# One load queue and a new order of steps in a linear-attention plus Mish feed-forward kernel

## The chip, the cores and the metric

The kernel runs on one core of a Trainium2 chip. The metric is the device time of one execution in microseconds, the median of the runs. A core has a matrix engine (TensorE, PE in the profile; PEld is its weight load), VectorE (DVE), ScalarE (ACT), GpSimd (POOL) and a sync engine (SP), which here only issues DMAs. ScalarE can issue DMAs too. SP and ScalarE each have a DMA queue of their own. Each engine carries out its own instructions in the order in which they were written and waits on semaphores for the others.

## The reference

```python
xn = layernorm(x)                                   # x: 2048 x 448, no gain or bias
q, k, v = split(xn @ wqkv)                          # 16 heads of 28
pq, pk = q @ w_phi, k @ w_phi                       # per head, 28 x 28
phi_q = concat(softmax(pq), softmax(-pq))           # 56 features per head
phi_k = concat(softmax(pk), softmax(-pk))
kv, z = phi_k.T @ v, sum(phi_k)                     # over all 2048 rows
o = (phi_q @ kv) / (phi_q @ z + 1e-6)
h = xn @ w1 + b1                                    # 448 -> 1792
out = x + o @ wo + mish(h) @ w2                     # mish(h) = h * tanh(softplus(h))
```

Inputs and output are bfloat16.

## The kernel before, in words

The 2048 rows are 16 tiles of 128 (t = 0 to 15), worked on in 8 pairs (u = t // 2). Everything stays in on-chip memory: x, the weights, the activations (actT) and exp(k), which lies in the half of actT that the second half of the feed-forward writes later.

The kernel is a list of steps. Each step has a short name and a function; the string ORDER names all steps in the order in which they are recorded, and a small recorder (Program) turns that list into one instruction list per engine, with a semaphore wait wherever a step reads or overwrites what another engine or a DMA produces. So ORDER alone decides the order of work on every engine and in every DMA queue. The last letter of some names says where a step runs: a for ScalarE, d for VectorE, p for POOL, m for a DMA transpose, s for SP's queue.

The steps, in the order of the data:

- Loads: lxA.Bs/a loads x tiles A to B-1; lkm and lvm the first 384 rows of the k and v columns of wqkv; lkt, in before, the last 64 rows of both, twice, to the lower and to the upper 64 partitions (Wkv[:, 3]); lqT0 to lqT3 the q columns by DMA transpose (WqT); lp w_phi (Wbd), lb b1, l1m and l1t w1, l2 w2, lo wo.
- Layer norm: stT statistics, rs (a pair) or rtT (a tile) the reciprocal deviation, xnT the normalised tile into one of four buffers xn0 to xn3, xtU the transpose of a pair into xnT. With xtUb or xtUa TensorE transposes and ScalarE and/or VectorE copy out; with xtUm a DMA does it.
- Folding w_phi into the projections: wtk0 and wtk1 turn the k weights on TensorE (L547), wmk0 and wmk1 multiply them by Wbd (L571) and copy the result to Wpk; qd copies the end of WqT once more, and wmq0, wmq1 make Wpq from it.
- Projections of a pair: kU, qU, vU. Each is 14 matmuls in three passes, A, B and H; two matmuls of 64 rows run side by side. A unit holds a pair of the eight PSUM banks until its result is copied out: exp(k) and exp(-k) by ScalarE (L609), exp(q) likewise (L682), v by ScalarE or VectorE (the copies all show as L509 or L511).
- Key normalisation: knU.S, a row sum and reciprocal on VectorE (L617, L619) and a scaling on POOL (L621) for each sign; kcU does the sum of both signs in one instruction (L627).
- kvU: 16 matmuls of a pair into kv, accumulated over all pairs; kvz masks the result and a DMA transposes it (KVZ). It needs all 16 scalings by POOL.
- eT transposes exp(q) of tile T by DMA (EqT); ndT makes numerators and denominators on TensorE, then a chain of seven VectorE instructions; otU transposes the result back.
- Feed-forward: fQ.C is half Q (tiles 0 to 7, or 8 to 15) of chunk C of w1, 14 matmuls in passes A, B and H, then Mish on ScalarE with another activation table (L703). gT is the product with w2, 14 matmuls (L828); wo the output projection (L845); a VectorE sum with x (L793) and stoU, sttT the stores.
- z12: 12 matmuls on zeros at the very start. pi, pw, pp, pv, pk: constants, masks and paddings by POOL.

Of the kernel before, what the change touches and what calls it, by code (L numbers as in the profile page):

```python
# [171 lines left out]
def _kernel(es, nc, A_x, A_wqkv, A_w_phi, A_wo, B_w1, B_b1, B_w2, out):  # L172
# [363 lines left out]
    def w_tr(h, eng):  # L536
# [7 lines left out]
        def tr(e):  # L544
            for c in range(2):
                for g in range(G):
                    ins = e.transpose(oT(c)[:, g, :], Wk[:, 2 * h + c, g * GP:(g + 1) * GP], ident[:])  # L547
# [432 lines left out]
```

## Time and profile before

| | |
|---|---|
| median of 3 runs | 153.9 us (153.81 to 154.15) |
| profiled execution | 153.96 us, of which the span of its instructions is 152.2 us |
| TensorE busy | 144.6 us (95%), 1541 matmuls |
| VectorE busy | 101.1 us (66%) |
| ScalarE busy | 75.7 us (50%) |
| POOL busy | 44.3 us (29%), all of it before 57 us |
| DMA moved | 17.22 MB, mean 113 GB/s |
| TensorE clock granted | 1.00 |

How to read it: shares are means over stages with different limits, and a busy TensorE says little where matmuls follow each other with waits that the modelled ends cover. What counts in a stage is the chain of work: which wait ended last there. Rows of the timeline merge instructions of one kind: start, time from the first start to the last end, how many; in brackets the idle time of the engine before and what ended it.

### The profile page before, as it was taken

How to read it: one execution, taken by the hardware profiler on the slowest of the kernel's cores; microseconds unless marked ns; L12 is line 12 of the kernel's file. 1: busy time of each engine (PE TensorE's matmuls, PEld its weight loads, DVE VectorE, ACT ScalarE, POOL GpSimd, SP SyncE). 2: the span in 40 equal slices, each digit the busy share in tenths (PEclk: the TensorE clock that was granted, in tenths of full speed). 3: DMA queues.
4: the chain of work that ended last, by engine and by line, in shares of the span. 5: the costliest groups of instructions: out<-in, count | busy, mean ns of one | idle time of the engine just before them, and what ended most of it. 6: DMA issues, size and time to landing. Idle time of an engine off the chain costs nothing.

```text
span 152.2 us, 3611 instructions
## 1 busy us (share of the span) xinstructions
PE 144.6 (95%) x1541; PEld 76.1 (50%) x1541; DVE 101.1 (66%) x223; ACT 75.7 (50%) x90; POOL 44.3 (29%) x65
## 2 busy tenths in 40 slices
PE   3978999989999979999999999999999999999993
PEld 1454545445444574445344455554544554559552
DVE  0699989599969903599606999535995999200721
ACT  3485999995995699778997730000500400000000
POOL 3385688969999950000000000000000000000000
PEclk9999999999999999999999999999999999999999
DMA  5995964989967243994399260500035000540204
GB/s 123 288 260 147 174 143 93 131 268 262 101 137 138 76 139 73 180 197 41 60 149 321 86 65 14 119 0 0 2 65 151 30 4 0 121 121 4 87 4 151
DMA packets 40436, 17.22 MB, mean 113 GB/s; under 512 B 34020, under 2 KB 39908, under 8 KB 40420
## 3 DMA queue, kind: packets, MB, share of 16 engines
q1 hardware_dynamic: 37548, 14.46, 46.9%
q10 hardware_dynamic: 2872, 2.53, 5.6%
q8 instruction: 12, 0.20, 0.5%
q14 instruction: 4, 0.03, 0.1%
HBM read 7.02 MB, written 1.84 MB: 58 GB/s over the span
## 4 chain that ended last, share of the span: by engine, by line
PE 78%; ACT 12%; DMA 4%; DVE 3%; issue 1%; ACTq 0%
PE PS L429 38%; PE PS L828 28%; PE PS L845 7%; DMA x_all<-in_A_x_dram 4%; ACT actT L609 3%; PE PS L723 2%; PE PS L650 2%; ACT actT L682 2%; ACT v_all L509 2%; DVE Sk L627 1%; ACT Wpq L509 1%; ACT Eq L682 1%; DVE v_all L511 1%; ACT Eq L509 1%; ACT Wpk L509 1%
## 5 line engine op out<-in xcount | busy, mean ns | idle before, releaser
L703 ACT ACTIVATE actT<-PS,b1T 128x1024 bf16<-128x1024 f32 x28 | 30.2, 1112 | 33.1 <-PE PS L429 33.0
L429 PE MATMUL PS<-xnT,W 64*128 64x512 bf16 x392 | 46.2, 376 | 0.0
L828 PE MATMUL PS<-W,actT 128*128 128x448 bf16 (+1 forms) x224 | 42.7, 351 | 0.0
L828 PEld LDWEIGHTS PS<-W,actT 128*128 128x128 bf16 x224 | 21.5, 98 | 20.3 <-issue 0.7
L429 PEld LDWEIGHTS PS<-xnT,W 64*128 64x128 bf16 x392 | 18.1, 94 | 21.0 <-ACT actT L703 0.4
L793 DVE TENSOR_TENSOR x_all<-PS,x_all 128x448 bf16<-128x448 f32 (+1 forms) x16 | 9.5, 616 | 20.3 <-PE PS L845 10.3
L621 POOL TENSOR_TENSOR actT<-actT,rSk 128x896 bf16<-128x896 bf16 x12 | 20.0, 1699 | 0.0
L609 ACT ACTIVATE actT<-PS 128x896 bf16<-128x896 f32 x16 | 13.7, 950 | 3.7 <-DVE stats L466 1.8
L429 PE MATMUL PS<-Wkv,xnT 64*128 64x448 bf16 x112 | 13.6, 349 | 0.6 <-DVE v_all L511 0.6
L429 PE MATMUL PS<-Wpk,xnT 64*128 64x448 bf16 x112 | 13.3, 349 | 0.5 <-ACT Wpk L509 0.5
L429 PE MATMUL PS<-Wpq,xnT 64*128 64x448 bf16 x112 | 12.7, 350 | 0.0
L466 DVE BATCH_NORM_STATS2 stats<-x_all 128x6 f32<-128x448 bf16 x15 | 9.2, 614 | 5.2 <-DMA x_all<-in_A_x_dram 5.2
L617 DVE TENSOR_REDUCE Sk<-actT 128x32 f32<-128x896 bf16 x12 | 12.5, 1043 | 0.0
L738 DVE COPY Sq<-PS 128x16 f32<-128x16 f32 x32 | 4.0, 167 | 12.5 <-PE PS L723 12.2
L749 DVE TENSOR_TENSOR xn<-v_all,rden 128x448 bf16<-128x448 f32 x16 | 10.0, 625 | 1.3 <-DMA Wkv<-xn 0.8
L746 DVE TENSOR_TENSOR v_all<-v_all 128x464 f32<-128x464 f32 x16 | 10.3, 642 | 0.6
L742 DVE TENSOR_TENSOR v_all<-PS,Sq 128x464 f32<-128x464 f32 x16 | 10.3, 642 | 0.5
L744 DVE TENSOR_TENSOR v_all<-PS,Sq 128x464 f32<-128x464 f32 x16 | 10.1, 630 | 0.0
L429 PEld LDWEIGHTS PS<-Wkv,xnT 64*128 64x128 bf16 x112 | 5.4, 94 | 6.0 <-DVE v_all L511 1.0
L682 ACT ACTIVATE actT<-PS 128x896 bf16<-128x896 f32 x10 | 8.4, 926 | 0.0
L429 PEld LDWEIGHTS PS<-Wpk,xnT 64*128 64x128 bf16 x112 | 5.3, 94 | 5.5 <-ACT Wpk L509 0.6
L429 PEld LDWEIGHTS PS<-Wpq,xnT 64*128 64x128 bf16 x112 | 5.1, 94 | 5.4 <-ACT actT L609 0.5
(85 smaller groups left out, 137.7 us busy)
## 6 DMA issues: line engine op xcount, KB each, us to landing
W<-in_B_w_dram SPq DMA_DIRECT2D x1, 1568.0 KB, 8.0
out_dram<-x_all SPq DMA_DIRECT2D x7, 224.0 KB, 2.2
W<-in_B_w_dram SPq DMA_DIRECT2D x1, 1344.0 KB, 7.2
x_all<-in_A_x_dram ACTq DMA_DIRECT2D x5, 224.0 KB, 4.1
Wo<-in_A_wo_dram ACTq DMA_DIRECT2D x2, 336.0 KB, 3.6
x_all<-in_A_x_dram SPq DMA_DIRECT2D x2, 224.0 KB, 4.9
W<-in_B_w_dram SPq DMA_DIRECT2D x2, 224.0 KB, 4.0
Wkv<-in_A_wqkv_dram SPq DMA_DIRECT2D x1, 336.0 KB, 4.2
```

The costliest lines, as they stand in the source:

```text
L429: ins = e.matmul(o, lhs(c, k), rhs(c, k), start=first and n == at[par][0], stop=last and n == at[par][-1])
L609: op("ACT", lambda e, s=s: e.activation(E_of(u)[:, s, :, :], two(b, D), ACT.Exp, scale=1.0 if s == 0 else -1.0), r=[pb(b), pb(b + 1)], w=[ ...
L617: op("DVE", lambda e: e.tensor_reduce(Sk[u][:, s, :], Eh(), AX.X, ALU.add), r=[("E", u, s)], w=[("Sk", u, s)], tag=f"Sk{u}.{s}")
L621: op("POOL", lambda e: e.tensor_tensor(Eh(), Eh(), ap_on(rSk[u][:, s, 0:1], [[1, 2 * H], [0, DH]]), ALU.mult), r=[("E", u, s), ("rSk", u, ...
L682: op("ACT", lambda e, s=s: e.activation(Eq_of(u)[:, :, s, :].rearrange("p i (h n) -> p i h n", n=64)[:, :, :, 0:QP], two(b, D).rearrange(" ...
L703: op("ACT", lambda e: e.activation(actT[:, q, fc, :], bank(b, 2), ACT.Mish, bias=b1T[:, fc:fc + 1]), r=[("b1T",), pb(b), pb(b + 1)], w=[(" ...
L742: op("DVE", lambda e: e.tensor_tensor(tv(t1[i]), num(0), sx(1), ALU.mult), r=[pb(b), pb(b + 1), ("Sq", i, 1)], w=[("t1", i)], tag=f"ta{t}")
L744: op("DVE", lambda e: e.tensor_tensor(tv(t2), num(1), sx(0), ALU.mult), r=[pb(b), pb(b + 1), ("Sq", i, 0)], w=[("t2",)], tag=f"tb{t}")
L746: op("DVE", lambda e: e.tensor_tensor(t1[i], t1[i], t2, ALU.add), r=[("t1", i), ("t2",)], w=[("t1", i)], tag=f"tc{t}")
L749: op("DVE", lambda e: e.tensor_tensor(o_sb[(t // 2) % 2][:, t % 2, :].rearrange("p (h d) -> p h d", d=DH), t1[i][:, :, 0:DH], ap_on(rden[i ...
L828: ins = e.matmul(bank(b)[:, 0:width(t)], act_of(fc, t), W2[:, fc, 0:width(t)], start=first and fc == 0, stop=last and fc == FC - 1)
L845: ins = e.matmul(bank(b)[:, 0:w], oT_of(u)[lo:hi, cc * P:(cc + 1) * P], Wo[lo:hi, cc, 0:w], start=first and n == at[par][0], stop=last and ...
```

## The change

Three edits, and a part that is only defined.

1. The tail of the weights. Before, the last 64 rows of the k and v columns came twice, 64 partitions of 896 columns each. Now the lower half gets k and v, the upper half v alone, and the turning of the k weights (w_tr, second half) takes the tail from the lower 64 partitions twice: eight transposes of 64 rows to 64 columns in place of four of 128 rows to 128 columns.
2. The queues. All loads of x, the k, v and q weights, w1, w2 and wo are in SP's queue; b1 and w_phi in ScalarE's.
3. ORDER is new as a whole.

New functions center, center_T, minus_rstd, v_early, k_early and q_early are defined and given step names (xc, ct, nr, v..e, v..f, k..c, q..c), of which none is in the new ORDER; tok_works, x_res, early_of serve them.

```diff
-pi lx1.2a pw table lx0.1s lx4.6a lx2.4a zero st1d lpa st5a st0d st4d st2d rs0p lvma rs2p lx6.8a xn0a xn1d lkms xn5p
-lkts xn4p lx8.10s lbs st3d z12 wtk0a rt2a wtk1d xt0b lqT3 rt3a wmk0d wmk1a pp b1 xt2b xn2d st8d lqT1 lqT2 lqT0 xn3d
...
+lx1.2s lx2.4s lx0.1s pw pi lx4.8s zero table pp z12 st1d st0d rs0p st2d lba st4d lkms xn1d rt4p lkts lpa st3a lvts
+st5a rt5a lvms xn0d xn4d b1 lx10.12s rs1p wtk0a lx12.14s xt0a lx8.10s xn5d wtk1d wmk0d xn3d lqT3 xt2b wmk1a xn2d lqT0
...
+    def load_kv_tail(i, eng):
+        lo, hi = HALF[i]
+        dst, src = (Wv, A_wqkv[384:448, 2 * D:3 * D]) if i else (Wkv, A_wqkv[384:448, D:3 * D])
+        dma(eng, lambda e: e.dma_start(dst[lo:hi, 3, :], src), w=[("Wt", i)], tag=f"ldWt{i}")
...
-        return [(name, 0), ("Wt", 0), ("Wt", 1)] if name in ("Wk", "Wv") else [(name, i) for i in range(3)]
+        return [(name, 0), ("Wt", 0)] + ([("Wt", 1)] if name == "Wv" else []) if name in ("Wk", "Wv") else \
+            [(name, i) for i in range(3)]
...
-                    ins = e.transpose(oT(c)[:, g, :], Wk[:, 2 * h + c, g * GP:(g + 1) * GP], ident[:])
+                    for lo, hi in HALF if h and c else ((0, P),):
+                        ins = e.transpose(oT(c)[:, g, lo:hi], Wk[0:hi - lo, 2 * h + c, g * GP:(g + 1) * GP],
+                                          ident[0:hi - lo, 0:hi - lo])
...
-        add(f"lkt{c}", load_tail, eng, "Wkv", Wkv, A_wqkv[:, D:3 * D])
+        for i, n in enumerate("kv"):
+            add(f"l{n}t{c}", load_kv_tail, i, eng)
```

What the new order does on the engines is shown at four places; the line numbers of the kernel after are its own. First SP's queue from its first load on, before:

```order
L273 DMA x_all<-in_A_x_dram 128x448
L276 DMA Wkv<-in_A_wqkv_dram 128x3x448
L281 DMA Wkv<-in_A_wqkv_dram 64x896 x2
L273 DMA x_all<-in_A_x_dram 128x896
L303 DMA b1_rows<-in_B_b1_dram 14x128
L285 DMA_TRANSPOSE WqT<-in_A_wqkv_dram 128x448 x4
L516 DMA_TRANSPOSE xnT<-xn1 128x7x128
```

And after:

```order
L286 DMA x_all<-in_A_x_dram 128x448
L286 DMA x_all<-in_A_x_dram 128x896
L286 DMA x_all<-in_A_x_dram 128x448
L286 DMA x_all<-in_A_x_dram 128x1792
L289 DMA Wkv<-in_A_wqkv_dram 128x3x448
L300 DMA Wkv<-in_A_wqkv_dram 64x896
L300 DMA Wkv<-in_A_wqkv_dram 64x448
L289 DMA Wkv<-in_A_wqkv_dram 128x3x448
L286 DMA x_all<-in_A_x_dram 128x896 x3
L303 DMA_TRANSPOSE WqT<-in_A_wqkv_dram 128x448 x4
L535 DMA_TRANSPOSE xnT<-xn1 128x7x128
```

The k weights move from second place to fifth, behind 896 KB of x, and the q weights' transposes stand behind eleven loads. Further on in SP's queue, behind the next three xnT transposes, the kernel before has two more of them and then the main part of w1; after, two transposes of exp(q) come first:

```order
L535 DMA_TRANSPOSE xnT<-xn0 128x7x128
L780 DMA_TRANSPOSE EqT<-actT 128x8x128 x2
L535 DMA_TRANSPOSE xnT<-xn1 128x7x128
L535 DMA_TRANSPOSE xnT<-xn3 128x7x128
L289 DMA W1<-in_B_w1_dram 128x3x1792
```

The two EqT rows are tiles 3 and 2 (pair 1); the two xnT rows behind them pairs 5 and 7.

Second, ScalarE from its first copy of turned key weights (Eq0) to the first exp(k) (L609), before, its DMA issues among them:

```order
L509 ACTIVATE Eq0<-PS 112x1024
L478 ACTIVATE lnv<-mv,eps_col 128x1
L480 ACTIVATE rstd<-lnv 128x1
L509 ACTIVATE xnT<-PS 128x384
L478 ACTIVATE lnv<-mv,eps_col 128x1
L480 ACTIVATE rstd<-lnv 128x1
L509 ACTIVATE Wpk<-PS 128x896
L509 ACTIVATE xnT<-PS 128x384
L273 DMA x_all<-in_A_x_dram 128x896 x2
L609 ACTIVATE actT<-PS 128x896 x2
```

And after (L699 is the first exp(k); L477 to L481 are the statistics of a tile, here tile 6):

```order
L528 ACTIVATE Eq0<-PS 112x1024
L528 ACTIVATE xnT<-PS 128x896
L528 ACTIVATE xnT<-PS 128x384
L528 ACTIVATE Wpk<-PS 128x896
L477 ACTIVATE junk1,mv<-x_all 128x448
L479 ACTIVATE rmean<-mv 128x1
L481 ACTIVATE junk1,mv<-x_all,rmean 128x448
L528 ACTIVATE v_all<-PS 128x32x28
L699 ACTIVATE actT<-PS 128x896 x2
```

Two pairs of logarithm and exponential for rstd left the stretch between Eq0 and Wpk; a set of statistics and the copy of v of pair 0 came in ahead of the first exp(k).

Third, TensorE from the turning of the key weights to the folding of q, before:

```order
L547 MATMUL PS<-ident,Wkv 112x128 x16
L504 MATMUL PS<-ident,xn 128x128 x7
L571 MATMUL PS<-Wbd,Eq 128x112 x16
L695 MATMUL PS<-ident,b_rows 128x14
L504 MATMUL PS<-ident,xn 128x128 x7
L429 MATMUL PS<-Wpk,xnT 128x448 x22
L429 MATMUL PS<-Wkv,xnT 128x448 x28
L571 MATMUL PS<-Wbd,WqT 128x112 x16
```

And after:

```order
L567 MATMUL PS<-ident,Wkv 112x128 x8
L523 MATMUL PS<-ident,xn 128x128 x7
L567 MATMUL PS<-ident,Wkv 112x128 x4
L567 MATMUL PS<-ident,Wkv 112x64 x8
L592 MATMUL PS<-Wbd,Eq 128x112 x8
L523 MATMUL PS<-ident,xn 128x128 x7
L592 MATMUL PS<-Wbd,Eq 128x112 x8
L448 MATMUL PS<-Wkv,xnT 128x448 x8
L448 MATMUL PS<-Wpk,xnT 128x448 x8
L448 MATMUL PS<-Wkv,xnT 128x448 x8
```

The first projection on TensorE is now v (Wkv) and not k (Wpk), and the two transposes of x stand between the halves of the key weights.

Fourth, POOL from the last of its mask steps (KVT) over its last normalised tile to its first scalings of exp(k), before:

```order
L354 MEMSET KVT 128x512
L498 TENSOR_SCALAR xn1<-x_all,rstd,shift 128x64
L498 TENSOR_SCALAR xn1<-x_all,rstd,shift 128x384
L621 TENSOR_TENSOR actT<-actT,rSk0 128x896 x2
L621 TENSOR_TENSOR actT<-actT,rSk1 128x896
L633 TENSOR_TENSOR actT<-actT,rSk3 128x896 x2
```

And after, from the last normalised tile to the first mask step (mask2):

```order
L517 TENSOR_SCALAR xn3<-x_all,rstd,shift 128x64
L517 TENSOR_SCALAR xn3<-x_all,rstd,shift 128x384
L711 TENSOR_TENSOR actT<-actT,rSk2 128x896
L711 TENSOR_TENSOR actT<-actT,rSk1 128x896
L711 TENSOR_TENSOR actT<-actT,rSk0 128x896
L711 TENSOR_TENSOR actT<-actT,rSk1 128x896
L364 MEMSET mask2 128x56
```

The mask steps moved behind the first four scalings. The order of the kv groups on TensorE is now pairs 4, 2, 0, 3, 1, 6, 7, 5 (before 2, 6, 1, 0, 5, 7, 4, 3), and ahead of them stand seven q units and a part of an extra feed-forward chunk (f0.1), where before the last q unit came after them. The copies of v of pairs 3, 4 and 5 went from VectorE to ScalarE, that of pair 7 from ScalarE to VectorE.

More of the change, by code (lines that the diff above doesn't have):

```diff
@@ new lines, in minus_rstd, with sign_rstd, v_early, then @@
+    def minus_rstd(u):
+        op("DVE", lambda e: e.tensor_scalar(nrstd[:, 2 * u:2 * u + 2], rstd[:, 2 * u:2 * u + 2], -1.0, 0.0, op0=ALU.mult, op1=ALU.add),
+           r=[("rstd", 2 * u), ("rstd", 2 * u + 1)], w=[("nr", u)], tag=f"nr{u}")
+    def sign_rstd(t, s):
+        return nrstd[:, t:t + 1] if s else rstd[:, t:t + 1]
+    def v_early(u, part, eng):
+        def then(b):
+            for i in range(2):
+                t = 2 * u + i
+                dst, src = v_all[:, u, i, :, 0:DH], bank(b + i)[:, 0:D].rearrange("p (h d) -> p h d", d=DH)
+                r, w = [pb(b + i), ("rstd", t)], [("v", u)] if i else [("vh", u)]
+                if eng == "ACT":
+                    op("ACT", lambda e, dst=dst, src=src, t=t: e.mul(dst, src, rstd[:, t:t + 1]), r=r, w=w, tag=f"vs{u}.{i}")
+                else:
+                    op("DVE", lambda e, dst=dst, src=src, t=t: e.tensor_scalar(dst, src, rstd[:, t:t + 1], 0.0, op0=ALU.mult,
+                                                                               op1=ALU.add), r=r, w=w, tag=f"vs{u}.{i}")
+        pair_part(f"v{u}", part, tok_works(u, Wv, True), x_res(u, True) + rows_of("Wv"), then)
@@ new lines, in k_early, with then @@
+    def k_early(u, part):
+        def then(b):
+            for s in range(2):
+                for i in range(2):
+                    t = 2 * u + i
+                    op("ACT", lambda e, s=s, i=i, t=t: e.activation(E_of(u)[:, s, i, :], bank(b + i)[:, 0:D], ACT.Exp,
+                                                                    scale=sign_rstd(t, s)),
+                       r=[pb(b + i), ("rstd", t), ("nr", u)], w=[("E", u, s)] if i else [("Eh", u, s)], tag=f"exkc{u}.{s}.{i}")
+        pair_part(f"k{u}", part, tok_works(u, Wp[1], True),
+                  x_res(u, True) + [("Wp", 1, h, c) for h in range(2) for c in range(2)], then)
@@ new lines, in q_early, with then @@
+    def q_early(u, part):
+        def then(b):
+            for s in range(2):
+                for i in range(2):
+                    t = 2 * u + i
+                    op("ACT", lambda e, s=s, i=i, t=t: e.activation(
+                        Eq_of(u)[:, i, s, :].rearrange("p (h n) -> p h n", n=64)[:, :, 0:QP],
+                        bank(b + i)[:, 0:D].rearrange("p (h n) -> p h n", n=QP), ACT.Exp, scale=sign_rstd(t, s)),
+                       r=[pb(b + i), ("Eqp", u % 3), ("rstd", t), ("nr", u)], w=[("Eq", u % 3, s)],
+                       tag=f"exqc{u}.{s}.{i}")
+        pair_part(f"q{u}", part, tok_works(u, Wp[0], True), x_res(u, True) + [("Wp", 0, c) for c in range(4)], then)
@@ L903, in _kernel @@
                 add(f"f{q}.{fc}{part}", ffn1, q, fc, part)
+    for u in range(4):
+        add(f"nr{u}", minus_rstd, u)
+        for eng, c in (("ACT", "a"), ("DVE", "d"), ("both", "b")):
+            add(f"ct{u}{c}", center_T, u, eng)
+        for part in "ABH":
+            add(f"v{u}{part}e", v_early, u, part, "ACT")
+            add(f"v{u}{part}f", v_early, u, part, "DVE")
+            add(f"k{u}{part}c", k_early, u, part)
+            add(f"q{u}{part}c", q_early, u, part)
+        for t in (2 * u, 2 * u + 1):
+            add(f"xc{t}d", center, t, "DVE")
+            add(f"xc{t}p", center, t, "POOL")
     add("kvz", kvz)
```

72 lines of the change are left out of this document (52 added, 20 removed).

## The prediction

> **What bounds the kernel now.** I read the page's shares first, then the chain of work that ended last, then the timeline of each engine where that chain leaves TensorE. The page and the chain, in order of time (start us, us, what):
>
> ```profile
> PE 144.6 (95%) x1541; PEld 76.1 (50%) x1541; DVE 101.1 (66%) x223; ACT 75.7 (50%) x90; POOL 44.3 (29%) x65
> PE 78%; ACT 12%; DMA 4%; DVE 3%; issue 1%; ACTq 0%
> ...
> 8.93 0.91 ACT Eq L509
> 9.84 0.19 ACT lnv L478
> ...
> 11.06 0.81 ACT Wpk L509
> ...
> 11.92 4.17 PE PS L429 x42
> ...
> 17.83 1.75 ACT Wpq L509 x4
> 19.58 3.24 ACT actT L609 x4
> ...
> 23.22 3.30 ACT actT L682 x4
> ...
> 28.14 0.81 ACT v_all L509
> ...
> 30.60 2.03 DVE Sk L627
> ...
> 33.20 0.96 DVE v_all L511
> ...
> 34.21 18.73 PE PS L429 x184
> 52.94 3.17 PE PS L650 x124
> 56.10 0.78 issue
> 56.88 0.29 PE PS L650 x4
> ...
> 149.27 0.56 DVE x_all L793
> ```
>
> Three parts. To 11.92 a serial start: x lands, is normalised, the key weights are folded (L547, L571), ScalarE moves them out (Wpk). From 11.92 to 34.2 ScalarE carries the chain, with a detour over VectorE at its end. From 34.2 TensorE runs without a break except the pause before the last kv group at 56.10. So time can come from an earlier start, from pauses before 57, and from nothing after 57 unless an edit adds a pause: TensorE's work is the same in both kernels, apart from the turned tail.
>
> Rates for what follows, from the timeline:
>
> ```profile
> 21.83 3.00 PE L429 MATMUL PS<-Wpq,xnT 64*128 64x448 bf16 x30
> 46.05 3.40 PE L429 MATMUL PS<-xnT,W 64*128 64x512 bf16 x30
> 34.21 0.74 PE L429 MATMUL PS<-Wkv,xnT 64*128 64x448 bf16 x6 [0.59 <-DVE v_all L511]
> 7.17 1.17 PE L547 MATMUL PS<-ident,Wkv 128*112 128x128 bf16 x16
> 9.90 0.96 PE L571 MATMUL PS<-Wbd,Eq 112*128 112x112 bf16 x16 [0.34 <-ACT Eq L509]
> 42.00 1.28 ACT L703 ACT_TABLE_LOAD   x1
> 45.03 9.99 POOL L621 TENSOR_TENSOR actT<-actT,rSk 128x896 bf16<-128x896 bf16 x6
> ```
>
> With a modelled end of 0.17 taken off a merged row, 30 matmuls of 448 take 2.83, so a k, q or v unit of 14 takes 1.32 (an A or B pass 0.57, H 0.19); a feed-forward unit of 14 matmuls of 512 takes 1.51. A kv group is 16/124 of 3.17 = 0.41. One POOL scaling of exp(k) is 1.67.
>
> **The change part by part.**
>
> *Dead code.* The new functions (center, v_early, k_early, q_early, minus_rstd) have no step in the order table, so no engine gets an instruction from them; early_of only names resources that nothing else writes. Cost 0.
>
> *Loads.* All loads of x and of the k and v weights now stand in SP's queue; ScalarE's keeps b1 and the four w_phi pieces. Wo's four loads move to SP too, behind the transpose of tile 6, some 30 us before the first wo: 0.
>
> ```profile
> 0.00:4.00 4.00, 1.70 (x5) 0.60 (x6) 0.37 (x1) 1.28 (x1) 1.35 (x10) 1.00 0.53 134
> 4.00:8.00 4.00, 4.00 (x22) 1.95 (x21) 2.66 (x8) 1.63 (x5) 1.68 (x4) 1.00 1.17 277
> 8.00:12.00 4.00, 2.55 (x40) 1.96 (x39) 3.90 (x14) 3.76 (x9) 2.73 (x7) 1.00 0.84 228
> x_all<-in_A_x_dram SPq DMA_DIRECT2D x1, 112.0 KB, 2.6
> Wkv<-in_A_wqkv_dram SPq DMA_DIRECT2D x1, 336.0 KB, 4.2
> 4.09 5.10 SPq L285 DMA_TRANSPOSE WqT<-in_A_wqkv_dram x4
> xnT<-xn SPq DMA_TRANSPOSE x6, 3.8
> ```
>
> The last columns of the first three rows are the clock, DMA share and GB/s. At these rates 536 KB have moved by 4.0 and 1,644 by 8.0. In the new order x tiles 0 to 7 are the first 896 KB: moved by 5.3, landed with some 0.5 of lag by 5.8. The key weights follow at 1,232 KB: 6.5, landed 7.0. That is 1.5 later than before (issued at 1.27, 4.2 to land), but TensorE could not use them earlier, since its warm-up runs to 7.17. The tail of V alone saves 56 KB, 0.2 of the queue. The bulk ends at 2,408 KB, landed near 11.9. SP's own issue is longer: eleven loads near 0.5, then four transposes of 1.27 (5.10/4) from about 6.2 to 11.3; the last would land near 14 to 15.5, and xT of pair 1, behind it, is issued when xn2 is ready at 11.7. [...] The rows leave the landing between 14 and 15.5; I take the middle, where nothing waits.
>
> *The turned tail.* Four transposes of 128 rows become eight of 64 rows. No row shows that shape; by the 16 above (0.063 from start to start) it costs between 0 and 4 x 0.063 = 0.25. I take 0.25. It lies under ScalarE's copy of the first half of the turned weights (0.91), which the next product needs anyway; uncovered it would cost 0.25.
>
> *The start, walked through.* x1 lands near 3.3, x2 and x3 by 3.8, x0 by 4.2, x4 to x7 by 5.8. ScalarE now takes the statistics of tiles 3 and 5.
>
> ```profile
> 5.42 0.58 ACT L458 ACTIVATE junk<-x_all 128x448 bf16<-128x448 bf16 x1 [2.87 <-DMA x_all<-in_A_x_dram]
> 6.92 0.19 ACT L462 ACTIVATION_READ_ACCUMULATOR junk<-x_all,rmean 128x1 f32 x1
> 24.75 1.07 DVE L617 TENSOR_REDUCE Sk<-actT 128x32 f32<-128x896 bf16 x1
> 27.11 5.01 POOL L621 TENSOR_TENSOR actT<-actT,rSk 128x896 bf16<-128x896 bf16 x3
> W<-in_B_w_dram SPq DMA_DIRECT2D x1, 1344.0 KB, 7.2
> ```
>
> One such set is 5.42 to 7.11 = 1.69: tile 3 from 3.85, tile 5 from 5.8 to 7.5, its logarithm and rstd (0.42, the two small steps of the chain) to 7.95. TensorE: warm-up to 7.17, first half of the key weights turned by 7.9, xT of pair 0 by 8.3, second half by 8.9. ScalarE: the turned half 7.95 to 8.85, xT of pair 0 to 9.75 (896 columns, taken as that same 0.9), xT of pair 2 to 10.3, Wpk 10.35 to 11.16. Between Eq and Wpk the chain of before has two pairs of ln and rstd, 0.8 in all; they are gone from this place, and that is where the start becomes earlier. TensorE: 9.75 to 10.13 the second product; then v of pair 0, which needs no folded weight, 10.13 to 10.9; then k of pair 0 at 11.2. Before, the stream began with k at 11.92 and v came after it. Start term: 1.8 earlier less the 0.35 hole = -1.45.
>
> *To the kv groups.* From k at 11.2 on TensorE has 23 units less the two v passes (29.6), six feed-forward units and the H and B passes of f0.1 (9.9) and the folding of q (16 matmuls, 0.8): 40.3, so kv could begin at 51.5. The same count for before gives 11.92 + 39.7 = 51.6, where the chain shows 52.94: 1.3 of waiting, of which the 0.59 behind the VectorE copy of v3 is the piece with a name. That copy stood behind a double reduction (2.03) which waited for exp(k3); in the new order ScalarE does v3 and no double reduction is left (two single ones take 2 x (1.07 + 0.35), less overlaps about the same as the double's 2.03 + 0.55). ScalarE allows it: exp of k0 begins 13.75, and counting 1.62 a pair (3.24/2), 0.82 a v and the two remaining Wpq copies it ends exp(k5) near 38.8 with all eight k, four q and five v, where before it came to the table load behind that work at 42.00, with one v fewer. What is late next: xT of pair 4 (issued 21.3 when POOL has done xn8, 3.8 to land: 25.1, wanted 25.1) and q4, whose bank waits for the copy of v4 (31.5, wanted 31.5).
>
> *The kv groups.* VectorE goes without a break from 9.5 (its steps to the first key sum add up to 14.2) and reaches it at 23.8 instead of 24.75; POOL begins at 25.15 instead of 27.11. It then has 16 x 1.67 and, now among them, the mask steps (2.2): 54.1. TensorE finishes the sixth group at 51.5 + 6 x 0.41 = 53.95, waits 0.15 for the seventh, ends the eighth at 54.9. Before: 57.17.
>
> *After that.* Before has 149.27 - 57.17 = 92.1 to the last sums. The new order has already done q3's A pass and 0.86 of f0.1, 1.4 more, so 90.7 are left: 54.9 + 90.7 = 145.6. I went through the waits there.
>
> ```profile
> 65.89 0.26 DVE L738 COPY Sq<-PS 128x16 f32<-128x16 f32 x2
> ...
> 66.73 0.63 DVE L744 TENSOR_TENSOR v_all<-PS,Sq 128x464 f32<-128x464 f32 x1
> ...
> 68.91 0.25 DVE L738 COPY Sq<-PS 128x16 f32<-128x16 f32 x2
> ```
>
> An nd chain takes VectorE 3.0 (65.89 to 68.91) and gives its bank back after 1.45; the tightest place is g10, which wants the bank of nd12 (0.5 spare). No new pause. The end is of the same form (g15, its sums, two stores).
>
> *Sum.* With no pause that I did not count: 145.6 against 149.27, -3.65. Before lost 1.3 + 0.95 on pauses in a stream with as many crossings between engines; five places of the walk above have less than 0.3 to spare. Between none of that and all of it (2.25) I take half: +1.1. Result -2.55 on the profiled execution (153.96, its span 152.2), which stands 0.06 above the median of 153.9: 151.4.
>
> **The rivals.**
>
> *POOL gives the lead back.* If VectorE is not ahead, POOL starts at 27.1 as before and ends its 28.9 at 56.0; kv ends 56.8, the end is 147.5: -1.8, with some 0.5 of small pauses 152.7. For it: VectorE is full from 9.5 on, any late x tile moves it. Against: even then most of the reordering stays.
>
> *The start does not move* (loads hidden anyway, ScalarE's chain as long as before): -3.65 + 1.45 + 1.1 = -1.1, 152.9. Against: the two ln/rstd pairs are out of the chain.
>
> *The clock falls back.*
>
> ```profile
> 2.31 5.03 PE L370 MATMUL PS<-zeros 128*128 128x512 bf16 x12 [2.31 <-POOL zeros L322]
> ```
>
> The warm-up's 12 matmuls take 0.42 each, twice the 0.216 that a pair of 512 columns costs later, though the clock column reads 1.00 there too. Between 7.2 and 11.2 the walk leaves TensorE pauses of some 0.7. If these let it fall back to the speed of the warm-up for about as long as that lasted (2.31 to 7.17, 4.9), half of it is lost: 2.4, so 153.8. Against: before had larger holes there, 1.45 idle between 8 and 12, and stayed fast. [...]
>
> *Slower: W1 behind the queue.* On SP, two transposes of exp(q1) now stand ahead of xT of pairs 5 and 7 and of W1's main part, and wait for exp(q1). I have that at 22.5, W1 issued at 27.6 and landed 7.2 later, 35.4 (unless it shares the queues), wanted at 36.5. All TensorE work stands behind it. If exp(q1) ends at 26.5 as before, W1 lands at 39.4, 2.9 too late: -2.55 + 2.9 is +0.35, the point from which this decides; with the two transposes landing beside it 1 more, 155. Against: exp(q1) is one place earlier in ScalarE's list.
>
> **How the numbers follow.** Forecast 0.57, POOL 0.15, start unmoved 0.11, clock 0.06, W1 0.11. What a measurement of this kernel can tell from no change is about 0.2%, 0.3 us. Faster: 0.57 + 0.15 + 0.11 = 0.83; same: the clock, 0.06; slower 0.11. The range goes from the sum with no uncounted pause (153.96 - 3.65 = 150.3) over POOL and the unmoved start to just short of the clock's case, 153.5.
>
> **What the profile after would show.** Right: key weights turned from about 7.2, first v matmul at 10.1 and first k at 11.2; POOL's first scaling near 25; kv ends near 55 to 56; no TensorE idle over 0.3 between 12 and 50; full from 57 to the last sums near 146.7. Wrong: a TensorE wait on a DMA of xnT or W1 between 20 and 37; the WqT double copy on VectorE held past 15.2 by the last WqT load; POOL starting at 27 or later; a clock below 1.00 after 7; a pause in the nd part.

## The result, and the profile after

The new kernel takes 155.94 us (median of 18 runs, 154.10 to 157.47); the kernel before, on the same chips, 153.91 us (153.45 to 154.34). The forecast was 151.4 us, so faster; it is slower, by 1.3% from median to median. The ratio 1.0053 (95% interval 1.0033 to 1.0074) leaves out, as disturbed, the nine runs whose mean granted clock was 0.978; the experiments below show that this clock is the new kernel's own doing, so the median of all runs is the figure to go by.

The 18 runs fall into three groups by their mean clock: 1.00 (four runs, mean 154.2), 0.989 (five, 155.2) and 0.978 (nine, 157.0). The profiled execution is one of the middle group: 155.42 us, span 153.5.

The shares of the chain on the page of the kernel after:

```profile
PE 84%; DMA 7%; DVE 6%; SPq 1%; issue 1%; DVEq 0%
```

The chain in order of time (start us, us, what):

```profile
2.66 6.42 DMA Wkv<-in_A_wqkv_dram
9.13 0.90 PE PS L567 x8
10.03 0.75 PE PS L523 x7
10.78 1.31 PE PS L567 x12
12.09 0.86 PE PS L592 x8
12.97 1.09 DVE Wpk L530
...
21.16 3.88 DMA xnT<-xn
25.04 0.14 issue
25.18 30.72 PE PS L448 x310
55.90 3.33 PE PS L740 x128
59.23 6.38 PE PS L448 x58
...
150.58 0.56 DVE x_all L883
```

ScalarE, which carried the chain of the kernel before from 16.11 to 30.60, is gone from it. The chain now has one long DMA near its start, the key weights, 6.42 us from issue to landing; after 12.97 it follows VectorE's list to the transpose that lands at 25.04. TensorE was held by that second part for 0.19 only, as its own rows show (in the bracket the idle time ahead of them), and by the first for 2.15:

```profile
9.13 0.90 PE L567 MATMUL PS<-ident,Wkv 128*112 128x128 bf16 x8 [2.15 <-DMA Wkv<-in_A_wqkv_dram]
...
13.66 0.93 PE L448 MATMUL PS<-Wkv,xnT 64*128 64x448 bf16 x8
14.73 0.55 PE L448 MATMUL PS<-Wpk,xnT 64*128 64x448 bf16 x4
...
25.18 0.36 PE L448 MATMUL PS<-Wpk,xnT 64*128 64x448 bf16 x2 [0.19 <-DMA xnT<-xn]
```

The first v comes at 13.66 (forecast 10.13), the first k at 14.73 (11.2; before 11.92). After that the only pause before the kv groups is 0.19. The table by stage has clock, DMA share and GB/s in its last columns:

```profile
4.00:8.00 4.00, 2.98 (x10) 1.03 (x8) 1.85 (x5) 1.98 (x6) 0.96 (x2) 1.00 0.92 249
8.00:12.00 4.00, 2.87 (x27) 2.69 (x27) 2.27 (x9) 3.62 (x9) 1.81 (x4) 0.67 1.28 283
12.00:16.00 4.00, 3.85 (x46) 2.55 (x47) 3.68 (x9) 2.57 (x6) 0.00 (x0) 0.90 0.44 86
```

Behind the 2.15 us in which TensorE stood still, the clock is at half for (4 x 0.33 + 4 x 0.10) / 0.5 = 3.4 us. From the first k to the last sums the new order takes 135.85 us against 137.35 before (149.27 - 11.92): it is 1.5 better, and its start is 2.8 worse. The sum, +1.3, is the difference of the last sums, 150.58 - 149.27. Of both figures 0.76 us is only a matter of counting: the first eight matmuls of v now stand ahead of the first k. At equal work the start is 2.0 worse and the rest 0.7 better.

### The profile page after: what moved, and what is told of

The parts are those of the page before. It is cut to its first block, busy times and chain, and to the rows that moved or that the text cites. A ratio compares the mean times of both kernels' runs of the same rounds, so it can differ in the third digit from the quotient of the medians.

```text
span 153.5 us, 3630 instructions
## 1 busy us (share of the span) xinstructions
PE 146.3 (95%) x1545; PEld 79.5 (52%) x1545; DVE 99.4 (65%) x223; ACT 79.3 (52%) x97; POOL 43.8 (29%) x66
## 4 chain that ended last, share of the span: by engine, by line
PE 84%; DMA 7%; DVE 6%; SPq 1%; issue 1%; DVEq 0%
PE PS L448 42%; PE PS L918 28%; PE PS L935 7%; DMA Wkv<-in_A_wqkv_dram 4%; DMA xnT<-xn 3%; PE PS L813 2%; PE PS L740 2%; DVE stats L485 2%; PE PS L567 1%; DVE xn L511 1%; SPq L286 1%; DVE Wpq L530 1%; DVE Wpk L530 1%; PE PS L592 1%; DVE mv L486 0%
## 5 line engine op out<-in xcount | busy, mean ns | idle before, releaser
L448 PEld LDWEIGHTS PS<-xnT,W 64*128 64x128 bf16 x392 | 19.1, 94 | 20.6 <-ACT actT L793 1.5
L711 POOL TENSOR_TENSOR actT<-actT,rSk 128x896 bf16<-128x896 bf16 x16 | 26.6, 1701 | 0.5 <-DVE rSk L709 0.3
L707 DVE TENSOR_REDUCE Sk<-actT 128x32 f32<-128x896 bf16 x16 | 16.5, 1034 | 0.0
L699 ACT ACTIVATE actT<-PS 128x896 bf16<-128x896 f32 x16 | 13.6, 920 | 0.2 <-PE PS L448 0.2
L448 PE MATMUL PS<-Wpq,xnT 64*128 64x448 bf16 x112 | 13.2, 349 | 0.0
L485 DVE BATCH_NORM_STATS2 stats<-x_all 128x6 f32<-128x448 bf16 x13 | 7.9, 611 | 5.2 <-DMA x_all<-in_A_x_dram 5.2
L448 PEld LDWEIGHTS PS<-Wpk,xnT 64*128 64x128 bf16 x112 | 5.8, 94 | 5.5 <-ACT actT L699 0.6
L448 PEld LDWEIGHTS PS<-Wkv,xnT 64*128 64x128 bf16 x112 | 5.9, 94 | 4.7
L448 PEld LDWEIGHTS PS<-Wpq,xnT 64*128 64x128 bf16 x112 | 5.8, 94 | 4.8 <-ACT v_all L528 0.2
```

Source lines behind the costliest of these rows:

```text
L448: ins = e.matmul(o, lhs(c, k), rhs(c, k), start=first and n == at[par][0], stop=last and n == at[par][-1])
L485: op("DVE", lambda e: e.bn_stats(stats[:, t, :], x_all[:, t, :]), r=[("x", t)], w=[("st", t)], tag=f"bn{t}")
L699: op("ACT", lambda e, s=s: e.activation(E_of(u)[:, s, :, :], two(b, D), ACT.Exp, scale=1.0 if s == 0 else -1.0), r=[pb(b), pb(b + 1)], w=[ ...
L707: op("DVE", lambda e: e.tensor_reduce(Sk[u][:, s, :], Eh(), AX.X, ALU.add), r=[("E", u, s)], w=[("Sk", u, s)], tag=f"Sk{u}.{s}")
L711: op("POOL", lambda e: e.tensor_tensor(Eh(), Eh(), ap_on(rSk[u][:, s, 0:1], [[1, 2 * H], [0, DH]]), ALU.mult), r=[("E", u, s), ("rSk", u, ...
```

## The experiments

All figures of a stage are from the profiled execution of that kernel. In the table "keys" is the first turning of key weights on TensorE, "first k" the first k matmul, "sums" the last sums with x; the runs are counted by their mean clock (1.00, which includes 0.998 and 0.999; 0.989; 0.978 or less). The profiled execution had lost clock in six kernels: after, x4-7 as two loads, keys ahead of x4-7, old order with new loads, new order with loads as before, and "the same in one queue". Their first k and sums include that loss.

| kernel | keys | first k | sums | median us (lowest to highest) | runs by clock |
|---|---|---|---|---|---|
| before | 7.17 | 11.92 | 149.27 | 153.91 | all 1.00 |
| after | 9.13 | 14.73 | 150.58 | 155.94 (154.10 to 157.47) | 4 / 5 / 9 |
| 24 warm-up matmuls | 10.20 | 14.40 | 151.30 | 155.61 (154.98 to 156.28) | 6 / 0 / 0 |
| 20 warm-up matmuls | 8.94 | 13.14 | 149.96 | 154.92 (154.64 to 155.27) | 6 / 0 / 0 |
| x6-7 behind the keys | 8.31 | 12.54 | 148.40 | 153.32 (152.88 to 154.00) | 12 / 0 / 0 |
| x4-7 as two loads | 9.35 | 15.95 | 152.17 | 154.85 (153.48 to 157.04) | 6 / 1 / 5 |
| keys ahead of x4-7 | 7.55 | 17.01 | 152.84 | 157.71 (157.41 to 158.21) | 0 / 0 / 5 |
| w_phi late | 8.24 | 12.78 | 148.28 | 154.26 (152.83 to 157.82) | 6 / 2 / 4 |
| x6-7 and w_phi late | 8.28 | 12.67 | 148.47 | 153.83 (153.15 to 154.46) | 12 / 0 / 0 |
| old order, new loads | 9.19 | 14.02 | 151.88 | 156.76 (154.96 to 157.38) | 2 / 4 / 0 |
| x on ScalarE's queue | 8.19 | 13.45 | 149.07 | 156.67 (154.01 to 157.17) | 3 / 1 / 8 |
| new order, loads as before | 7.40 | 16.10 | 153.01 | 157.54 (155.63 to 158.52) | 1 / 0 / 5 |
| tail edit alone | 6.74 | 11.81 | 149.28 | 153.93 (153.55 to 154.40) | 12 / 0 / 0 |
| two queues, steps to fit | 6.35 | 12.17 | 147.56 | 153.12 (152.25 to 153.66) | 11 / 0 / 0 |
| the same in one queue | 6.77 | 12.95 | 150.00 | 153.62 (152.63 to 154.79) | 11 / 1 / 0 |
| folding first | 6.67 | 12.40 | 148.48 | 153.56 (152.93 to 153.99) | 12 / 0 / 0 |

The theory after the result: the key weights land 2 us late because 896 KB of x stand ahead of them, and TensorE's wait for them drops its clock. The rivals: the new order of steps makes the start long whatever the loads do; the clock falls for a cause outside this kernel.

### The clock

```diff
-... zero table pp z12 st1d ...
+... zero table pp z12 z12 st1d ...     (24 warm-up matmuls)
+... zero table pp z12 z8 st1d ...      (20 warm-up matmuls)
```

> The kernel after with 24 instead of 12 matmuls on zeros at the start, nothing else. Theory A (the key weights land at 9.1 in place of 5.5, TensorE stands idle from 6.8 to 9.1 and its clock falls back to half for none, one or two stretches of some 3.4 us, each worth 1.7 us): the 24 matmuls reach to about 9.4, the clock reads 1.00 in every run, all runs lie between 153.9 and 154.6, first v matmul near 12.5 in place of 13.66. Rival B (the new order itself is slower, the clock is a by-product): the runs stay spread from 154 to 157.5.

> The kernel after with 20 warm-up matmuls in place of 12, so that the warm-up ends at about 9.0, as the key weights land, and not at 10.1 as with 24. If the pause of 2.15 us before the key weights is what lowers the clock: 1.00 in all runs, spread under 1.2 us, key weights turned from 9.1 to 9.2, first v near 12.4, k near 13.5, 153.9 to 154.5 us. If the clock falls for a cause that does not lie in the pause: the same three groups as the kernel after, 154.1 to 157.5, median near 156.

With both the clock is 1.00 in all runs, and the spread shrinks from 3.4 us to 1.3 and 0.6. So the pause lowers the clock: nothing but matmuls on zeros was added. Against a cause outside this kernel stands that the kernel before, on the same chips, never read below 0.999 in any run beside these experiments. The level was missed in both. With 24 the warm-up itself ran to 10.16, past the landing of the weights. With 20 the key weights are turned at 8.94 and the first v comes 3.12 later, at 12.06; in the profile of after that stretch takes 13.66 - 9.13 = 4.53. The half clock cost 1.4 there. But part of it is lost again:

```profile
2.31 6.50 PE L389 MATMUL PS<-zeros 128*128 128x512 bf16 x20 [2.31 <-POOL zeros L341]
8.74 0.18 PE L785 MATMUL PS<-ident,b_rows 14*128 14x14 bf16 x1
8.94 0.65 PE L567 MATMUL PS<-ident,Wkv 128*112 128x128 bf16 x8
...
12.06 0.93 PE L448 MATMUL PS<-Wkv,xnT 64*128 64x448 bf16 x8
...
28.67 1.31 PE L448 MATMUL PS<-Wpk,xnT 64*128 64x448 bf16 x12 [0.94 <-DMA xnT<-xn]
```

The last row is the wait for xT of pair 4, which the prediction had named as "late next" with nothing to spare; with 24 matmuls it is 0.99 at 29.97.

### What stands ahead of the key weights in the queue

```diff
-lx1.2s lx2.4s lx0.1s pw pi lx4.8s zero ... lkms xn1d rt4p lkts lpa st3a lvts
+lx1.2s lx2.4s lx0.1s pw pi lx4.6s zero ... lkms xn1d rt4p lkts lx6.8s lpa st3a lvts      (x6-7 behind the keys)
+lx1.2s lx2.4s lx0.1s pw pi lx4.6s lx6.8s zero ... lkms xn1d rt4p lkts lpa st3a lvts      (x4-7 as two loads)
+lx1.2s lx2.4s lx0.1s pw pi lkms lkts lx4.8s zero ... xn1d rt4p lpa st3a lvts             (keys ahead of x4-7)
```

> The kernel after with the load of x4-7 in two halves, x4-5 where it was and x6-7 behind the key weights' tail, all in SP's queue. Theory A with one queue served in order: x4-5 lands near 6.4 in place of 7.6 and the key weights near 8.2 in place of 9.1; the idle time before them shrinks to 1.3, fewer runs lose the clock; median 154.3, fastest 153.3. If the order within the queue does not matter: the key weights still land near 9, 155.9.

> The kernel after with x4 to x7 as two loads of 224 KB in place of one of 448, both still ahead of the key weights. If the key weights are late because of the 896 KB that stand before them: they land near 9.1 as before the edit, TensorE stands for about 2 us, the clock falls in most runs, 155 to 157 us. If it is the single large load (its long pieces, its slow first ones) that holds the queue up: they land near 8.3 as when x6-7 stood behind them, and 153.1 to 153.8 us.

> The kernel after with the key weights and their lower tail ahead of the load of x4 to x7, which stays one load of 448 KB; the same queue, nothing else moved. By place in the queue: key weights land at 6.8 to 7.5 and TensorE does not wait for them, but x4 to x7 land at 8.3 to 8.8, and with the statistics of tile 5 on ScalarE ahead of the copy of the key weights (2.2 us from landing to that copy) the copy begins at 10.5 to 11.0 and the first v comes at 12.9 to 13.5: the start stays late, 154 to 156 us. If the key weights alone set the start: first v at 10.6 to 11.5 and 152 to 153 us.

TensorE's row of the key weights, first with x6-7 behind them, then with x4 to x7 as two loads ahead of them:

```profile
8.31 0.65 PE L567 MATMUL PS<-ident,Wkv 128*112 128x128 bf16 x8 [0.68 <-DMA Wkv<-in_A_wqkv_dram]
```

```profile
9.35 0.80 PE L567 MATMUL PS<-ident,Wkv 128*112 128x128 bf16 x8 [2.21 <-DMA Wkv<-in_A_wqkv_dram]
```

Splitting the load alone changes nothing (9.35 against 9.13); putting 224 KB of it behind the key weights brings them 0.82 earlier. That is 280 GB/s (a KB here has 1024 bytes), and this profile moved 273 GB/s from 4 to 8 us, so it is about those bytes. How far a single profile can be trusted shows in the three kernels with the same loads: the key weights land near 9.1 in after, 9.3 with 24 and 8.9 with 20 warm-up matmuls. It is place, not form. And 2.6 us in the median come of it, for the clock stays up as well; against the four runs of after that kept their clock (154.2) it is 0.9. This kernel beats the one before, ratio 0.9957 (0.9936 to 0.9978).

The third one shows the limit. The key weights go ahead of all of x4 to x7, are turned at 7.55, and it is the slowest of all: the clock fell in all five runs, and 157.71 us lies above both forecasts. ScalarE and TensorE in that kernel:

```profile
9.36 0.58 ACT L477 ACTIVATE junk<-x_all 128x448 bf16<-128x448 bf16 x1 [3.52 <-DMA x_all<-in_A_x_dram]
...
11.52 1.00 ACT L528 ACTIVATE Eq<-PS 112x1024 bf16<-112x1024 bf16 x1
```

```profile
7.55 0.65 PE L567 MATMUL PS<-ident,Wkv 128*112 128x128 bf16 x8 [0.21 <-DMA Wkv<-in_A_wqkv_dram]
11.04 0.93 PE L523 MATMUL PS<-ident,xn 128*128 128x128 bf16 x7 [2.83 <-DVE xn L511]
```

x4 to x7 now land at 9.36; the statistics of tiles 4 and 5 stand in VectorE's and ScalarE's lists ahead of the normalised x and of the copy of the key weights, so both wait, and TensorE with them. In this order of steps the start needs x0 to x5 and the key weights, whichever comes last; x6 and x7 are the only bytes ahead of them that nobody is waiting for.

```diff
-... lkts lpa st3a lvts
+... lkts st3a lvts lps                                  (w_phi late)
+... lx4.6s ... lkts lx6.8s st3a lvts lps                (x6-7 and w_phi late)
```

> The kernel after with the four w_phi loads (448 pieces of 56 bytes) moved from ScalarE's queue to SP's, behind the tail of v. Theory C (the small pieces of the other queue, which run from 3.0 to 7.3, hold up the bulk in between): x4-7 lands by 6.2 in place of 7.6, the key weights by 7.8 in place of 9.1, median 154.3. If they do not matter: x4-7 still at 7.6, 155.9 with the same spread, or a little later because w_phi itself lands after 9.5.

> The kernel after with x6-7 behind the key weights and with the four w_phi loads behind the v tail in SP's queue, the two edits together. If both are bytes or pieces ahead of the key weights and add up (0.8 and 0.9): key weights land at 7.4 to 7.7, TensorE idle under 0.4, v at 10.6 to 11.0, k at 11.7 to 12.1, 152.4 to 152.9 us with the clock at 1.00 in all runs. If ScalarE's chain from the landing of x4-5 over the statistics of tile 5 to the copy of the key weights sets the start already: no better than the split alone, 153.1 to 153.5.

Taking w_phi's four loads of 6.1 KB out of the way brings the key weights from 9.13 to 8.24, as much as the 224 KB of x6-7. The two together bring no more (8.28): they do not add up. In that profile two limits meet: the first half of the key weights is turned at 8.93, after a wait of 1.73 for them, and ScalarE is through with tile 5 and free to copy it at 8.96. So the second theory of that expectation held in kind (no better than the split alone), though the time, 153.83, is 0.3 above its range. Why the landing stays at 8.3 is open. Single profiles of equal loads differ by 0.4, as said, but that does not bridge a missing 0.8. Open too is why the clock stayed up in all twelve runs of the one and not in six of the other; the profiled executions, both at 1.00, do not show the pauses of the runs in which it fell.

### Loads, order and tail apart

The kernel before with the new distribution of loads and its own order (a / stands for the end of a line; the loads of x10 to x15 on the third line moved too):

```diff
-pi lx1.2a pw table lx0.1s lx4.6a lx2.4a zero st1d lpa ... lvma rs2p lx6.8a xn0a xn1d lkms xn5p / lkts xn4p lx8.10s lbs st3d
+pi lx1.2s pw table lx2.4s lx0.1s lx4.8s zero st1d lba lpa ... rs2p xn0a xn1d lkms xn5p / lkts lvms xn4p lx10.12s lx12.14s lx8.10s st3d
```

> The kernel before with its own order of steps and its own double tail, only the loads moved as in the change: all x and k, v weights in SP's queue, x0 to x7 ahead of the key weights; b1 and w_phi alone in ScalarE's. If the load queue is what costs: key weights land near 9.1, TensorE stands idle for 1.5 to 2.2 us after its warm-up, the first k comes at 13.5 to 15, the granted clock falls below 1.00 in some runs, and the time is 155.3 to 157.5 us. If the load queue is neutral and the order costs: 153.6 to 154.3.

```profile
9.19 1.97 PE L547 MATMUL PS<-ident,Wkv 128*112 128x128 bf16 x16 [2.59 <-DMA Wkv<-in_A_wqkv_dram]
...
14.02 1.31 PE L429 MATMUL PS<-Wpk,xnT 64*128 64x448 bf16 x12 [0.49 <-ACT Wpk L509]
```

156.76 us: the loads alone cost 2.9 us in the median. The whole change costs 2.0, so the rest of it gives about 0.9 back; in the profiles, from the first k on, it was 0.7 at equal work. One of its two runs at clock 1.00 took 156.88, which nothing here explains.

```diff
-lkts xn4p        (before, with the new code of the tail)
+lkts lvts xn4p
```

> The kernel before, its order and its queues, with only the edit on the tail: lower half k and v, upper half v alone, eight transposes of 64 rows in place of four of 128. Priced by the rows of the new kernel (12 matmuls in 0.75 us, 0.063 each, so four more cost 0.25) and by 56 KB less (0.2 of a queue): between -0.2 and +0.3 us, no difference that the runs can tell, 153.7 to 154.2. If the tail edit were a part of the loss: 154.5 or more.

Ratio 1.0011 (0.9991 to 1.0032): nothing. The twelve turnings of the second half take 0.75 us where the clock is full (from 9.36 on in the kernel with x6-7 behind the keys), 0.063 each, as the prediction had priced them.

```diff
-lx1.2s lx2.4s lx0.1s pw pi lx4.8s zero ...
+lx1.2a lx2.4a lx0.1s pw pi lx4.8a zero ...      (x on ScalarE's queue, b1 behind it)
```

> The kernel after with the loads of x1, x2-3 and x4-7 issued by ScalarE's queue, ahead of its activation table; everything else in place. Theory A: the key weights land by 5.5 to 6 as in before, TensorE turns them right after its warm-up at 7.2 and stays busy enough to keep clock 1.00; x4-7 lands near 7.2, so the copies of the turned weights on ScalarE still start near 9.9 behind the statistics of tile 5; 153.3 (152.7 to 154.0). If instead the queue does not matter and only the order of bytes does: the key weights land near 9 again, 155.9 with the same spread.

```diff
-lx1.2s lx2.4s lx0.1s pw pi lx4.8s ... lba ... lpa st3a lvts / st5a rt5a lvms xn0d xn4d b1 ...
+lx1.2a lx0.1s pw pi lx4.6a lx2.4a ... lkms ... lkts lpa st3a lvts / st5a lx6.8a rt5a lvms xn0d xn4d lbs ... wmk1a b1 ...
```

> The order of steps after, with the loads shared out as before: x1, x4-5, x2-3, x6-7 and w_phi in ScalarE's queue, x0 and the key weights at the head of SP's (b1 behind the v weights, its transpose behind wmk1). If the late start of the new kernel is only the key weights standing behind 896 KB of x: key weights are there when the warm-up ends at about 7.2, v of pair 0 at 10.2 to 10.6, k at 11.3 to 11.7, and with the 41.1 us from there to the kv groups that the other kernels in this order took, the end comes at 151.9 to 152.4 us with the clock at 1.00 in all runs. If the new order of steps makes the start long whatever the loads do (ScalarE's statistics of tiles 3 and 5 ahead of the copy of the key weights): k not before 12.5 and 153.3 us or more.

In the first of the two b1 came behind x in ScalarE's queue, and its transpose, which stands ahead of the key weights on TensorE, held them until 8.19. The key weights themselves landed by 5.8 (issued at 1.27, 4.5 to land), as theory A had it; but nine of twelve runs lost clock, the median is 156.67, and with b1 in the way the time speaks for neither theory. The second was my clearest miss. With the loads as before (the main part of the v weights stays in SP's queue), the key weights are there at 7.40, and it takes 157.54 us:

```profile
9.76 0.56 PE L523 MATMUL PS<-ident,xn 128*128 128x128 bf16 x7 [1.36 <-DVE xn L511]
10.16 0.91 PE L567 MATMUL PS<-ident,Wkv 128*112 128x128 bf16 x12
12.16 0.93 PE L592 MATMUL PS<-Wbd,Eq 112*128 112x112 bf16 x8 [1.09 <-ACT Eq L528]
```

That distribution lands x4-5 first and x2-3 at 7.34; the new order has ScalarE take tile 3 and then tile 5 ahead of its copy of the key weights, so the copy begins at 11.10. Order of steps and order of loads belong together; neither of the two old halves fits the other's new one.

### A better start

Two queues again, and the first steps in the order in which these loads land:

```diff
-lx1.2s lx2.4s lx0.1s pw pi lx4.8s zero table pp z12 st1d st0d rs0p st2d lba st4d lkms xn1d rt4p lkts lpa st3a lvts
-st5a rt5a lvms xn0d xn4d b1 lx10.12s rs1p wtk0a lx12.14s xt0a lx8.10s xn5d wtk1d wmk0d xn3d lqT3 xt2b wmk1a xn2d lqT0
+lx1.2a lx0.1s pw pi lx4.6a lx2.4a zero table pp z12 st1d st0d rs0p lkms st4d xn1d lkts lpa xn0d rt4p lvts st5a rt5a lvms st2d
+st3d xn4d rs1p lx6.8s lbs lx10.12s wtk0a lx12.14s xt0a lx8.10s wtk1d xn5d wmk0d xn3d lqT3 xt2b wmk1a b1 xn2d lqT0
```

> The kernel after with the first loads shared by two queues again (x1, x4-5, x2-3 and w_phi in ScalarE's; x0, key weights, v weights, x6-7 and the rest in SP's), and with its first steps put in the order in which these loads land: normalising x1 and x0 ahead of the statistics of tiles 2 and 3, both of those on VectorE, ScalarE with tile 5 alone ahead of the copy of the key weights, b1 turned after the folding. If one queue keeps the 16 DMA engines less busy than two (204 to 282 GB/s from 4 to 6 us in the five kernels with one queue, 319 to 348 in the three with two) and the rest of the new order is sound: key weights turned at 7.2 to 7.5, the copy of them on ScalarE from about 8, first v at 10.2 to 10.8, first k at 11.1 to 11.8, kv from 52.2 to 53.0, the clock at 1.00 in all runs and 151.4 to 152.6 us, faster than both kernels. If what the start loses is a matter of ScalarE and VectorE steps and not of the queue: v not before 11.4 and 153.2 us or more, like the split of the x load in one queue.

```profile
6.35 0.61 PE L567 MATMUL PS<-ident,Wkv 128*112 128x128 bf16 x8
7.26 0.56 PE L523 MATMUL PS<-ident,xn 128*128 128x128 bf16 x7 [0.30 <-DVE xn L511]
7.66 0.91 PE L567 MATMUL PS<-ident,Wkv 128*112 128x128 bf16 x12
9.31 0.55 PE L592 MATMUL PS<-Wbd,Eq 112*128 112x112 bf16 x8 [0.74 <-ACT xnT L528]
...
11.11 0.93 PE L448 MATMUL PS<-Wkv,xnT 64*128 64x448 bf16 x8
```

153.12 us, ratio 0.9952 (0.9934 to 0.9971): the lowest median, faster than both kernels, though above the 151.4 to 152.6 expected. Its interval overlaps that of the small edit that put x6-7 behind the keys (153.32), so the new steps are not shown to add anything to it. The key weights are no longer what it waits for; between them and the first v stand ScalarE's and VectorE's steps. The same steps with all these loads in SP's queue (x1, x0, x4-5, key weights, x2-3, v weights, x6-7), and the version that folds first:

> The steps of the two-queue version unchanged, but its loads all in SP's queue again, in the order of need of these steps (x1, x0, x4-5, key weights, x2-3, v weights, x6-7), b1 and w_phi alone in ScalarE's. If one queue keeps the DMA engines less busy: 200 to 285 GB/s from 4 to 6 us against 334, x2-3 or the key weights 1 us or more later, first v at 11.9 to 12.8, 153.8 to 154.8 us. If the new steps made the gain and the queue does not matter: 152.9 to 153.4 like the two-queue version.

> The two-queue version with three more moves, to take out the waits that its start showed: the warm-up in two steps of 11 and 1, so that PSUM banks are handed out as in the kernel after; both halves of the folding ahead of the transpose of pair 2; VectorE copies the second half of the key weights and the first half of the fold before it normalises tiles 4 and 5. If the start is now set by ScalarE and VectorE steps and no longer by loads: the folding from 8.4 to 8.6 in place of 9.3, first v at 9.7 to 10.2, first k near 11.0 to 11.3, 151.6 to 152.4 us. If what is gained there is only handed on to the transposes by DMA further on (pairs 1, 4 or 5 late, a wait of 0.5 to 1.0 between 15 and 30 us): no better than the two-queue version, 152.8 to 153.3.

In one queue it is 153.62 us, ratio 0.9970 (0.9944 to 0.9997), with the key weights turned at 6.77. The intervals overlap: the second queue is worth some 0.5 us or less. What the key weights need is their place. Folding first brought the first v to 10.13, the very figure of the prediction, and no gain: the transpose of pair 2, moved behind it, made the first k later than in the version before (12.40 against 12.17), and the time 153.56.

## Why the prediction was wrong

The step that failed is the term of the loads, x4 to x7 "landed with some 0.5 of lag by 5.8" and the key weights "6.5, landed 7.0", hidden under the warm-up. They landed at 7.6 and 9.1. The rest of the walk stood on it, and the clock, put at nothing in the sum, fell with it.

- *Loads.* The rates 134, 277 and 228 GB/s were those of the kernel before, taken over for another queue. Up to 4 us they nearly fit (125 GB/s against 134), then they don't. From 4 to 6 us, columns as above, before first, then after:

```profile
4.00:6.00 2.00, 2.00 (x6) 0.74 (x5) 1.72 (x5) 0.58 (x2) 0.62 (x2) 1.00 1.08 332
```

```profile
4.00:6.00 2.00, 2.00 (x6) 0.74 (x5) 1.36 (x4) 1.63 (x5) 0.41 (x2) 1.00 0.82 204
```

  And the load of x4 to x7 among the DMA issues of after (KB each, us from issue to landing):

```profile
x_all<-in_A_x_dram SPq DMA_DIRECT2D x1, 448.0 KB, 5.4
```

  x4 to x7 take 5.4 from an issue at 2.2: 7.6, not 5.8. The key weights come at 9.13, not 7.0. The half microsecond of "lag" put on top of a sum of bytes, an estimate that no row gave, was too little: in this queue a load of 336 KB behind 896 KB took 6.42 from issue. Bytes moved and bytes landed are two things, and only rows of landing price the second; before had one at 4.2 for these very weights, as the second load of its queue, and none for the fifth. By the rates of after (125, 204 and then 294 GB/s) the bytes up to the end of the key weights had moved near 7.3: of the 2.1 that the landing was late, 0.8 is rate and 1.3 is lag (0.1 of the first is that the sum set KB of 1024 bytes against rates in thousands). Why a load lands 1.8 behind its bytes there, no run shows. And 204 is the low end: the same loads gave 229 and 254 in the profiles with 24 and 20 warm-up matmuls.
- *One queue or two:* from 4 to 6 us the ten kernels with these loads in one queue moved 204 to 292 GB/s, five of those with two 319 to 348. The times show little of that: at equal steps the second queue gave some 0.5 us or less (153.12 against 153.62), which the runs do not tell from nothing. The miss was in the order of the bytes, not in their number of queues.
- *Start.* 3.53 us late at the first v: 9.13 - 7.2 = 1.93 by the loads, 1.4 by the clock, 0.2 the rest. In the sum's own terms the start was put at -1.45 and came out at 13.66 - 11.92 + 0.3 (the hole ahead of the first k) = +2.0. Key weights in time would not have been enough: x4 to x7 landed 1.9 later than forecast too, and with tile 5 behind them ScalarE was free for the first copy at 9.91, not at 7.95; it began at 10.13.
- *The clock* was a rival with 0.06, and against it stood that before had larger holes and stayed fast. Those holes were several; now it is one of 2.15, and 14 of 18 runs lost clock. The forecast let the landing of the weights decide the start but never asked what TensorE does if they are late: the rival had hung on a pause of 0.7, so the two misses came as one.
- *Dead code, turned tail:* no row, and no difference (1.0011). Right.
- *To the kv groups:* 40.3 forecast from the first k, 41.17 measured (14.73 to 55.90) with 0.19 of waiting; 41.14 with x6-7 behind the keys. The work was counted 0.7 to 0.8 short.
- *kv groups:* 128 matmuls in 3.33 without a pause against 3.4. Right. POOL began at 29.52, not 25.15, 0.8 more than the late start explains, and TensorE did not wait for it; with w_phi late it did, 0.15.
- *After that:* 90.7 forecast, 150.58 - 59.23 = 91.35 measured, without a new pause. So the +1.1 allowed for uncounted pauses met an error of 1.5 that was mostly uncounted work.
- *Slower by W1:* TensorE never waited for it. The side was right, the mechanism another.

Without the 3.53 the last sums would have come at 147.05, if nothing else had waited (with 20 warm-up matmuls xT of pair 4 then did, 0.94); forecast was 146.7. "Start does not move" (152.9) named the right place, and stopped at zero where a loss was possible: a moved load was bounded from one side only.

## What to carry to other kernels

When loads are put in one queue, price each by where its last byte stands and by rows of landing at that depth, and sort by the first step that waits, not by tile number: here 224 KB that nobody needed yet were worth 2.6 us, most of it through the clock. Order of loads and order of steps are one edit; halves of two tuned pairs were worse than either pair. And ask of every wait on TensorE near its start not only how long it is, but whether the clock survives it (here 2.15 us in the profiled execution, and 14 of 18 runs lost clock); a few idle-time matmuls are a cheap test (with 8 or 12 more, 12 of 12 runs kept it).

## What the runs showed of the hardware

The loss of clock came in steps: mean clocks of 1.00, 0.989 and 0.978 are 0, 3.4 and 6.8 us at half clock (0.011 x 153.5 / 0.5, and twice that). In the profiled execution of after it is one stretch, 0.50 from 9.38 to 12.79, so 3.4 us, behind a pause of 2.15 that followed a warm-up which had just ended.

The traces show where the clock fell. In the profile of after the matmuls of the warm-up take 634 ns each, and 380 from about 5.96 on: there the clock rises, by their lengths (the clock column reads 1.00 before it too). Half clock begins at 9.38, 3.42 behind that. In all six profiled executions that lost clock the rise and the fall lie 3.4 us apart, or 6.8 (5.15 and 11.98 for the steps of two queues in one). The last 3.4 us ahead of the fall held 1.57 to 2.24 us of idle time on TensorE, in one pause or in several: in the new order with the loads as before it was 1.36 and the first 0.55 of the pause of 1.09. The rise lies between 5.08 and 8.20 in the profiles with 12 warm-up matmuls, and these end between 6.44 and 7.60; so the pause behind them is longer behind an early rise and shorter behind a late one (1.73 behind a warm-up that ended at 6.44, 0.68 behind one that ended at 7.53, with the keys turned at 8.28 and 8.31), though nothing in the warm-up differs. That this sorts the 18 runs into their three groups is likely and not shown, as one of them alone was profiled.

In the run of x4 to x7 as two loads, at 0.978, a pause of 2.21 left this (clock in the third column from the end):

```profile
8.00:10.00 2.00, 0.66 (x9) 0.66 (x10) 1.54 (x6) 1.08 (x4) 1.64 (x4) 0.93 1.09 303
10.00:12.00 2.00, 2.00 (x21) 1.87 (x18) 0.00 (x0) 1.76 (x2) 0.00 (x0) 0.50 1.55 229
12.00:14.00 2.00, 2.00 (x23) 1.94 (x22) 1.60 (x2) 0.23 (x2) 0.00 (x0) 0.50 0.87 167
14.00:16.00 2.00, 2.00 (x16) 0.93 (x16) 1.97 (x8) 1.74 (x4) 0.00 (x0) 0.50 0.00 0
```

A pause of 1.73 (x6-7 and w_phi late) left the clock at 1.00, and one of 1.53 (the steps of two queues in one) cost it once in twelve runs. So the idle time alone does not decide it, and where the limit lies, no run here settles. And 448 pieces of 56 bytes in another queue held the key weights back by 0.9 us in one comparison (9.13 against 8.24), as much as 224 KB in their own, and by nothing in another (8.31 against 8.28).
